# Diagonal matrices in the transposes of the first 12 attention units, and six instead of five weight steps per unit

## The chip, the cores and the metric

The kernel runs on one core of a Trainium2 chip. Its time is what the device needs for one execution, in microseconds (us). The engines of the core work side by side, each through its own queue in order: TensorE (PE in the profile; its weight loads are shown apart as PEld), VectorE (DVE), ScalarE (ACT), GpSimd (POOL) and SyncE (SP, which here only issues transfers).

## The reference

Top-32 attention over 8 batches, 8 heads, 576 positions and head size 64, then a SwiGLU block on the 4608 rows of 512 that it gives. All that is computed:

```python
scores = scale * np.matmul(q, k.transpose(0, 1, 3, 2))
kth = np.partition(scores, -top_k, axis=-1)[..., -top_k:-top_k + 1]
scores = np.where(scores >= kth, scores, -1000000000.0)
scores = scores - np.max(scores, axis=-1, keepdims=True)
attn = np.exp(scores)
attn = attn / (np.sum(attn, axis=-1, keepdims=True) + 1e-09)
x = np.matmul(attn, v)                    # then heads side by side: (4608, 512)
g = x @ w_gate                            # 512 x 1536
y = (g / (1 + np.exp(-g)) * (x @ w_val)) @ w_out
```

The three weight matrices come as 64-bit floats and are rounded to 32 bits on the chip.

## The kernel before

**Units.** The attention is cut into 160 units in this order: batch, block of 128 queries, pair of heads. There are four pairs (`NHP` = 4) and five query blocks for a batch, the last of 64 queries; a unit of that last block counts as one head, since two units share the 128 partitions. So a batch has 16 full units and 4 of one head, and units 0 to 11 are the first three query blocks of batch 0.

**One turn of the main loop** (`for n in range(NU + 3)`) works on several units at once:

- `select(n)`, on DVE: for each head four rounds of MAX8 (L347) with three MATCH_REPLACE8 between them (L351), 14 instructions for a full unit. It writes the working tile `e` of the unit, of which there are three; so unit n waits until unit n-3 has been transposed.
- `weigh(n-1)`, on ACT: Prelu (L374) and Exp (L379) make the unnormalized weights `e` and their sums `tot`; the exponent's offset comes from `shift` on POOL (L362).
- `normalize(n-1)`: the reciprocal of the sums on DVE (L393), then `e` times that reciprocal. For the first 12 units POOL does it for both heads (L399, two instructions of 128x576); from unit 12 on ACT takes the first head (L397).
- `turn(n-2)`, on PE: nine transposes of 128x128 into PSUM (L412), in chunks of four, one and four; the one in the middle holds the last 64 keys of both heads. ACT copies the chunks to the tile `et` (L413).
- in even turns `scores(n+1)` and `scores(n+2)` (PE L325, ACT L330) and, between them, `values` of units n-4 and n-3 (PE L448, ACT L465, which writes `xT`, the input of the feed-forward block).

**The feed-forward block** works on 18 blocks of 256 rows. The first three (`HALVED`) are computed in halves of 128 rows (L517; L569 is the output product of block 0). Its matmuls are put between the attention's steps in pieces: `share(n)` says how much a turn may issue, and `piece()` gives a piece or nothing. A piece of the first two blocks is given only when its weights are ready (`sure`) and its tokens are done.

**Weights.** There are 36 pieces of weights, each of 128x512. Each takes three steps: a transfer from HBM into one of four buffers `w`; three passes on ACT (L117, L119, L120); then a shift on DVE (L124) and two passes on POOL (L125, L126). The generator `weights()` interleaves them, so that a piece is finished by every second step. `dve(k)` lets DVE's selection proceed and, while the six selection instructions of its last three calls go by, adds to `due`; a step of the weights is issued when `due` reaches 1. With 5/6 for each of the six that is five steps per full unit, so 2 or 3 pieces by turns.

**Order.** Nothing is scheduled by a planner. At the end the kernel ties each instruction of PE, DVE, ACT and POOL to the one before it on the same engine, so each of these runs in the order in which the program emits. SP's queue is not tied; its transfers stand in the order of the built program.

Of the kernel before, what the change touches and what calls it, by code (L numbers as in the profile page):

```python
# [9 lines left out]
ALU = mybir.AluOpType  # L10
FP32 = mybir.dt.float32
# [4 lines left out]
P = 128  # L16
# [9 lines left out]
def kernel(  # L26
# [37 lines left out]
    nc = tc.nc  # L64
    B, H, S, D = q.shape
    DM, DFF = w_gate.shape
    J = S // P
    JP = J * P
    R = S - JP
    NHP = H // 2  # L70
# [4 lines left out]
    NBLK = B * S // BLK  # L75
    HALVED = 3
    AHEAD = 8 * NHP
    scale = 1.0 / float(D) ** 0.5
    assert D == 64 and R == 64 and H * D == DM and DM == 512 and B * S % BLK == 0

# [6 lines left out]
    ffn = ctx.enter_context(tc.tile_pool(name="ffn", bufs=2))  # L87
# [3 lines left out]
    ident = consts.tile([P, P], FP32, name="ident")  # L91
# [113 lines left out]
    def rounding(n):  # L205
        for _ in range(n):
            next(weight, None)
# [74 lines left out]
    state = {}  # L282

    def n_heads(qt):

        return 1 if qt == J else 2

    def scores(n):
        b, qt, hp = units[n]
        slab = preps[b * NHP + hp]  # L290
        sc = work.tile([P, 2 * S], FP32, tag="sc", name="sc", bufs=3)
        halves = [slice(0, D), slice(D, P)]
        half = S // 2

        def bank():
            return ps_t.tile([P, 512], FP32, tag="t", name="s")


        if qt == J:
            both = (slab, preps[b * NHP + hp + 1])  # L300
            banks = []
            for i in range(2):
                k0 = R + i * half
                two = [bank(), bank()]
                banks += [(i + 2 * u, ps) for u, ps in enumerate(two)]
                for u, (sl, ps) in enumerate(zip(both, two)):
                    for hh, d in enumerate(halves):
                        nc.tensor.matmul(  # L308
                            ps[halves[hh ^ u], 0:half],
                            sl[d, S + R : S + 2 * R],  # L310
                            sl[d, k0 : k0 + half],
                        )
            yield
            for i, ps in banks:
                nc.scalar.mul(sc[:, i * half : (i + 1) * half], ps[:, 0:half], scale)
            state[n + 1] = dict(sc=sc, at=S)
        else:
            q0 = S + 2 * R + qt * P
            banks = []
            for i in range(2):  # L320
                for hh, d in enumerate(halves):
                    ps = bank()
                    banks.append((i + 2 * hh, ps))
                    k0 = (1 - hh) * R + i * half
                    nc.tensor.matmul(  # L325
                        ps[:, 0:half], slab[d, q0 : q0 + P], slab[d, k0 : k0 + half]
                    )
            yield
            for i, ps in banks:
                nc.scalar.mul(sc[:, i * half : (i + 1) * half], ps[:, 0:half], scale)  # L330
        state[n] = dict(sc=sc, at=0)

    def select(n):

        nh = n_heads(units[n][1])
        sc = state[n]["sc"]
        m = small.tile([P, 2, TOP_K], FP32, tag="m", name="m")
        heads = [slice(t * S, (t + 1) * S) for t in range(nh)]
        at = state[n]["at"]
        from_ = [slice(at + t * S, at + (t + 1) * S) for t in range(nh)]  # L340
        e = work.tile([P, 2 * S], FP32, tag="e", name="e", bufs=3)
        state[n] |= dict(m=m, e=e, heads=heads, source=from_)
        cur = sc
        rounds = TOP_K // 8
        for r in range(rounds):
            for t, hs in enumerate(from_):
                nc.vector.max(m[:, t, 8 * r : 8 * r + 8], cur[:, hs])  # L347
                yield
            if r < rounds - 1:
                for t, hs in enumerate(heads):  # L350
                    nc.vector.match_replace(  # L351
                        e[:, hs], m[:, t, 8 * r : 8 * r + 8], cur[:, from_[t]], LOWEST
                    )
                    yield
                cur, from_ = e, heads
# [11 lines left out]
    def weigh(n):  # L367
# [10 lines left out]
        for t, hs in enumerate(heads):  # L378
# [3 lines left out]
            )  # L382
        if n < AHEAD:
            nc.scalar.add(tot[:, 0 : len(heads)], tot[:, 0 : len(heads)], EPS)
        st["tot"] = tot

    def normalize(n):
        st = state[n]
        tot, e, heads = st.pop("tot"), st["e"], st.pop("heads")
        nh = len(heads)  # L390
        for t in range(nh if n >= AHEAD else 0):
            nc.vector.tensor_scalar_add(tot[:, t : t + 1], tot[:, t : t + 1], EPS)
        nc.vector.reciprocal(tot[:, 0:nh], tot[:, 0:nh])  # L393
        yield
        for t, hs in enumerate(heads):
            if t == 0 and n >= 3 * NHP:
                nc.scalar.mul(e[:, hs], e[:, hs], tot[:, t : t + 1])  # L397
            else:
                nc.gpsimd.tensor_tensor(  # L399
                    e[:, hs], e[:, hs], tot[:, t : t + 1].to_broadcast([P, S]), ALU.mult  # L400
                )

    def turn(n):

        last = units[n][1] == J
        e = state[n].pop("e")
        et = work.tile([P, 2 * J + 1, P], FP32, tag="et", name="et")
        for c0, cn in ((0, J), (J, 1)) if last else ((0, J), (J, 1), (J + 1, J)):
            ps = ps_t.tile([P, 512], FP32, tag="t", name="etps")
            for c in range(cn):  # L410
                k0 = S - P if last and c0 == J else (c0 + c) * P
                nc.tensor.transpose(ps[:, c * P : (c + 1) * P], e[:, k0 : k0 + P], ident[:])  # L412
            nc.scalar.copy(  # L413
                et[:, c0 : c0 + cn, :],
                ps[:, 0 : cn * P].rearrange("p (c j) -> p c j", c=cn),
            )
            if c0 == J:
                yield
        state[n]["et"] = et
# [67 lines left out]
    def flush(queue):  # L487
        while queue:
            queue.pop(0)()
# [314 lines left out]
    def fetch(n):  # L804

        b, qt, hp = units[n]
        i = b * NHP + hp
        if qt == 0:
            yield from prep(i)
        if qt == J and i + NHP < len(pairs):  # L810
            load(i + NHP)

    def share(n):
# [9 lines left out]

        beside = 5.8 if n < AHEAD else 6.25
        least = 2.0 if n >= 3 * NHP and n % 2 == 0 else 0.0
        return max(least, beside * n_heads(units[n][1]) / 2 - others)

    def scored(n):

        ahead = [n + 1] if n < 2 else [] if n % 2 else [n + 1, n + 2]  # L830
        return [m for m in ahead if m < NU and (units[m][1] < J or m % 2 == 0)]
# [11 lines left out]
    def run(steps):  # L843
        for _ in steps:
            pass
# [23 lines left out]
    due, steps = [2.0], []  # L869
    for n in range(NU + 3):  # L870
        nh = n_heads(units[n][1]) if n < NU else 1
        topk = select(n) if n < NU else no
        norm = normalize(n - 1) if 0 <= n - 1 < NU else no
        nxt = [scores(m) for m in scored(n)]
        ahead = fetch(n + 3 if n else 2) if n + 3 < NU else no

        def dve(k, beside=True):

            for _ in range(k * nh):
                next(topk, None)  # L880
                due[0] += 5 / 6 if beside else 0
                if due[0] >= 1 and not (n == 0 and len(steps) == 5):
                    due[0] -= 1
                    steps.append(n)
                    rounding(1)

        if n >= NU - NHP:
            credit[0] = 8.0
        else:
            credit[0] = min(credit[0] + share(n), share(n) + 1)  # L890
        flush(on_act)
        flush(on_pool)
        if nxt and (n < 2 or len(nxt) > 1):
            run(nxt.pop(0))
        summed = finish_units(valued(n)) if valued(n) else no
        next(summed, None)
        if nxt:
            next(nxt[0])
        early[0]()
        if 0 <= n - 1 < NU:  # L900
            weigh(n - 1)
        run(summed)
        if nxt:
            run(nxt.pop())


        dve(2, beside=False)
        if n == 0:
            run(ahead)
            load(3)  # L910
            ahead = fetch(3)
        if n < NHP:
            load_v(n)
        pieces(2)
        flush(on_act)
        dve(1)
        dve(1)
        if 0 <= n - TURN < NU:
            run(turn(n - TURN))

        flush(on_pool)
        next(ahead, None)
        pieces(1)
        next(ahead, None)
        dve(1)
        pieces(1)
        if n < AHEAD:
            run(topk)
        run(norm)
        run(topk)  # L930
        if n < NU:
            shift(n)
        pieces(6)
# [50 lines left out]
```

## Time and profile before

| what | value |
|---|---|
| median of 3 runs | 1713.59 us (1713.14 to 1713.67) |
| profiled execution | 1712.03 us |
| its span, first to last instruction | 1710.2 us |
| PE busy | 1647.4 us, 96% |
| DVE busy | 1476.5 us, 86% |
| ACT busy | 1259.5 us, 74% |
| POOL busy | 799.0 us, 47% |
| mean granted clock of PE | 0.978 |

A row of the tables by line gives the line, the engine, the operation, the tiles, the count, the busy time and the mean of one. A row of the timeline gives the start, the length, the engine, the line and, in brackets, the idle time before it and what ended it. PE is shown in records: a transpose of `e` is one record, a matmul of 32-bit data is two. Turn n ends on DVE with the reciprocal of unit n-1; in the first stretch those stand at 34.5, 44.9, 56.6, 67.3, 79.1, 89.4, 100.8, 111.8, 123.4, 135.8, 148.6, 160.5 and 172.3 us for n = 1 to 13.

### The profile page before, as it was taken

The numbers are of one execution on the slowest core, as the hardware profiler recorded it, in microseconds if no ns is written. First come the engines' busy times: TensorE is split into PE (matmuls) and PEld (weight loads), VectorE is DVE, ScalarE is ACT, GpSimd is POOL, SyncE is SP. The second block draws the span as 40 slices with busy tenths as digits, with TensorE's granted clock in tenths as the row PEclk, the third lists the DMA queues.
The fourth block names the chain that finished last, engine by engine and source line by source line (L and its number), as shares of the span: only waits on it lengthen the run. The fifth ranks groups of instructions, "written<-read, shape, count | busy, mean of one in ns | idle before, by whom it ended". The sixth has DMA issues, their size and how long they took to land.

```text
span 1710.2 us, 32128 instructions
## 1 busy us (share of the span) xinstructions
PE 1647.4 (96%) x11600; PEld 1398.2 (82%) x11600; DVE 1476.5 (86%) x3311; ACT 1259.5 (74%) x2901; POOL 799.0 (47%) x914
## 2 busy tenths in 40 slices
PE   5588999999999999999999999999999999999999
PEld 3477698987888887888888888888888888888887
DVE  7999899998989899997999989998999979999400
ACT  7899887877767787768676887777777778676531
POOL 4798545352444425353535334444344433535434
PEclk6699999999999999999999999999999999999999
DMA  7533120003000030001200030000400011000000
GB/s 210 139 112 99 29 72 2 14 1 79 22 13 1 15 86 14 1 8 42 51 14 1 13 74 27 2 13 2 98 1 13 2 44 29 13 2 13 1 13 13
DMA packets 109310, 59.74 MB, mean 35 GB/s; under 512 B 88544, under 2 KB 96992, under 8 KB 109152
## 3 DMA queue, kind: packets, MB, share of 16 engines
q1 hardware_dynamic: 108016, 57.37, 12.9%
q8 instruction: 91, 1.49, 0.4%
q14 instruction: 67, 0.55, 0.1%
q10 hardware_dynamic: 1136, 0.33, 0.1%
HBM read 48.23 MB, written 9.44 MB: 34 GB/s over the span
## 4 chain that ended last, share of the span: by engine, by line
PE 88%; DVE 5%; ACT 4%; DMA 1%; POOL 1%; issue 1%; SPq 0%; POOLq 0%; ACTq 0%
PE f L604 37%; PE x_ps L670 10%; PE av L448 9%; PE s L325 8%; PE y_ps L670 8%; PE etps L412 7%; PE f L517 6%; DVE m L347 2%; DVE e L351 2%; PE kqps L271 1%; PE o_ps L569 1%; PE s L308 1%; ACT e L379 1%; DVE size L124 1%; ACT e L374 0%
## 5 line engine op out<-in xcount | busy, mean ns | idle before, releaser
L347 DVE MAX8 m<-e 128x8 f32<-128x576 f32 x864 | 617.9, 755 | 3.3
L351 DVE MATCH_REPLACE8 e<-m,e 128x576 f32<-128x576 f32 x576 | 425.4, 748 | 0.0
L604 PE MATMUL f<-xT,wg 128*128 128x256 f32 x1440 | 335.9, 382 | 1.3 <-ACT xT L465 1.3
L604 PE MATMUL f<-xT,wv 128*128 128x256 f32 x1440 | 331.4, 380 | 0.0
L604 PEld LDWEIGHTS f<-xT,wg 128*128 128x128 f32 x1440 | 268.9, 190 | 49.0 <-issue 13.1
L604 PEld LDWEIGHTS f<-xT,wv 128*128 128x128 f32 x1440 | 268.2, 190 | 37.5 <-issue 3.8
L640 POOL TENSOR_TENSOR h<-h,half_g 128x512 f32<-128x512 f32 x90 | 114.7, 1275 | 349.2 <-ACT h L639 349.2
L330 ACT ACTIVATE sc<-s 128x288 f32<-128x288 f32 x512 | 170.4, 431 | 105.2 <-PE s L325 104.6
L413 ACT COPY et<-etps 128x512 f32<-128x512 f32 (+1 forms) x448 | 183.6, 486 | 66.0 <-PE etps L412 65.6
L379 ACT ACTIVATE e<-e,bias 128x576 f32<-128x576 f32 x288 | 221.7, 780 | 12.7 <-POOL bias L362 9.7
L374 ACT ACTIVATE e<-sc,m 128x576 f32<-128x576 f32 x288 | 212.3, 792 | 0.6 <-DVE m L347 0.5
L351 DVE MATCH_REPLACE8 e<-m,sc 128x576 f32<-128x576 f32 x288 | 212.6, 748 | 0.0
L412 PE MATMUL etps<-ident,e 128*128 128x128 f32 x1312 | 178.2, 280 | 33.7 <-POOL e L399 15.0
L347 DVE MAX8 m<-sc 128x8 f32<-128x576 f32 x288 | 204.0, 747 | 7.5 <-ACT sc L330 7.5
L412 PEld LDWEIGHTS etps<-ident,e 128*128 128x128 f32 x1312 | 156.2, 144 | 54.7 <-POOL e L399 19.2
L645 POOL TENSOR_TENSOR h<-h,val 128x512 f32<-128x512 f32 x90 | 114.8, 1275 | 155.0 <-ACT val L644 152.4
L325 PE MATMUL s<-kqT 64*128 64x288 f32 x1024 | 169.2, 441 | 13.7 <-ACT sc L330 7.5
L399 POOL TENSOR_TENSOR e<-e,tot 128x576 f32<-128x576 f32 x140 | 161.1, 1154 | 28.5 <-DVE tot L393 28.2
L448 PE MATMUL av<-et,v 128*64 128x128 f32 (+1 forms) x2560 | 158.0, 268 | 0.0
L448 PEld LDWEIGHTS av<-et,v 128*64 128x64 f32 x2560 | 137.7, 140 | 5.9 <-ACT kqT L268 2.7
L325 PEld LDWEIGHTS s<-kqT 64*128 64x128 f32 x1024 | 94.2, 190 | 58.3 <-issue 18.4
L397 ACT ACTIVATE e<-e,tot 128x576 f32<-128x576 f32 x148 | 119.1, 805 | 21.7 <-DVE tot L393 21.6
(86 smaller groups left out, 2249.1 us busy)
## 6 DMA issues: line engine op xcount, KB each, us to landing
v<-in_v_dram SPq DMA_DIRECT2D x32, 256.0 KB, 3.3
kq_in<-in_k_dram SPq DMA_DIRECT2D x63, 128.0 KB, 2.8
kq_in<-in_q_dram SPq DMA_DIRECT2D x63, 128.0 KB, 2.9
w<-in_moe_w_gate_dram SPq DMA_DIRECT2D x12, 512.0 KB, 3.8
w<-in_moe_w_val_dram SPq DMA_DIRECT2D x12, 512.0 KB, 3.8
w<-in_moe_w_out_dram SPq DMA_DIRECT2D x12, 512.0 KB, 3.5
out_dram<-o SPq DMA_DIRECT2D x38, 128.0 KB, 2.4
out_dram<-o SPq DMA_DIRECT2D x16, 256.0 KB, 2.5
```

The lines of the kernel that those rows point to most:

```text
L325: nc.tensor.matmul(ps[:, 0:half], slab[d, q0 : q0 + P], slab[d, k0 : k0 + half])
L330: nc.scalar.mul(sc[:, i * half : (i + 1) * half], ps[:, 0:half], scale)
L347: nc.vector.max(m[:, t, 8 * r : 8 * r + 8], cur[:, hs])
L351: nc.vector.match_replace(e[:, hs], m[:, t, 8 * r : 8 * r + 8], cur[:, from_[t]], LOWEST)
L374: nc.scalar.activation(e[:, hs], sc[:, at], AF.Prelu, bias=m[:, t, TOP_K - 1 : TOP_K], scale=-1.0, alpha=SMALL,)
L379: nc.scalar.activation(e[:, hs], e[:, hs], AF.Exp, bias=bias[:, t : t + 1], scale=-1.0 / SMALL, accum_out=tot[:, t : t + 1],)
L399: nc.gpsimd.tensor_tensor(e[:, hs], e[:, hs], tot[:, t : t + 1].to_broadcast([P, S]), ALU.mult)
L412: nc.tensor.transpose(ps[:, c * P : (c + 1) * P], e[:, k0 : k0 + P], ident[:])
L413: nc.scalar.copy(et[:, c0 : c0 + cn, :], ps[:, 0 : cn * P].rearrange("p (c j) -> p c j", c=cn),)
L448: nc.tensor.matmul(av[d, i, 0:ql], weights_, moving, start=c == (0 if last else J), stop=c == (J if last else J - 1),)
L604: nc.tensor.matmul(ps[:, i, :], w[:, kc, m * P : (m + 1) * P], x[:, kc, :], start=(kc == 0), stop=(kc == KC - 1),)
L670: nc.tensor.matmul(ps, lhsT, T[i][m], start=m == 0, stop=m == MQ - 1)
```

## The change

In the first 12 units (`SCALED`) `e` is no longer multiplied by the reciprocal sums. POOL makes two diagonal matrices instead, the identity times the reciprocal of each head (one instruction of 128x256), and the transposes of these units become matmuls of `e` with them, which scale while they transpose. The middle chunk holds keys of both heads, so it becomes two matmuls of 64 columns each. The matrices of four units share one tile, in the slot of the output tile `o`. And `due` gets 1 for each selection instruction, so that a full unit issues six steps of the weights, three pieces, until the 36 pieces are through.

```diff
+    SCALED = 3 * NHP
...
+    scaling = []
+
     def normalize(n):
...
         nc.vector.reciprocal(tot[:, 0:nh], tot[:, 0:nh])
         yield
+        if n < SCALED:
+            if not scaling:
+                scaling.append(ffn.tile([P, 4, 2, P], FP32, tag="o", name="diag", bufs=1))
+            st["diag"] = diag = scaling[0][:, n % 4]
+            nc.gpsimd.tensor_tensor(
+                diag,
+                ident[:].unsqueeze(1).to_broadcast([P, 2, P]),
+                tot[:].unsqueeze(2).to_broadcast([P, 2, P]),
+                ALU.mult,
+            )
+            return
         for t, hs in enumerate(heads):
...
         e = state[n].pop("e")
+        diag = state[n].pop("diag", None)
...
-                nc.tensor.transpose(ps[:, c * P : (c + 1) * P], e[:, k0 : k0 + P], ident[:])
+                at = slice(c * P, (c + 1) * P)
+                if n >= SCALED:
+                    nc.tensor.transpose(ps[:, at], e[:, k0 : k0 + P], ident[:])
+                elif c0 == J:
+                    for t in range(2):
+                        d = slice(t * R, (t + 1) * R)
+                        nc.tensor.matmul(
+                            ps[d, at],
+                            e[:, k0 + t * R : k0 + (t + 1) * R],
+                            diag[:, t],
+                            start=True,
+                            stop=True,
+                        )
+                else:
+                    nc.tensor.matmul(
+                        ps[:, at], e[:, k0 : k0 + P], diag[:, c0 // J], start=True, stop=True
+                    )
...
-                due[0] += 5 / 6 if beside else 0
+                due[0] += 1 if beside else 0
```

## The prediction

> **What bounds the kernel now.** The page's first block gives PE 96% and the clock row shows where the rest is: in the first slices.
>
> ```profile
> PE 1647.4 (96%) x11600; PEld 1398.2 (82%) x11600; DVE 1476.5 (86%) x3311; ACT 1259.5 (74%) x2901; POOL 799.0 (47%) x914
> ...
> PEclk6699999999999999999999999999999999999999
> ```
>
> So I read the busy times by stretch next (after each stretch its length, then PE, PEld, DVE, ACT, POOL).
>
> ```profile
> 0.00:43.00 43.00, 24.20 (x97) 16.08 (x97) 31.07 (x70) 33.21 (x76) 19.78 (x27) 0.68 0.78 209
> 43.00:86.00 43.00, 24.63 (x154) 18.41 (x155) 43.00 (x91) 37.86 (x85) 34.06 (x32) 0.64 0.50 138
> 86.00:128.00 42.00, 34.59 (x305) 31.50 (x306) 42.00 (x90) 38.75 (x85) 38.62 (x33) 0.92 0.38 113
> 128.00:171.00 43.00, 37.04 (x310) 34.36 (x309) 42.14 (x82) 39.84 (x89) 38.03 (x35) 0.92 0.32 99
> 171.00:214.00 43.00, 42.59 (x309) 27.85 (x308) 38.40 (x81) 34.78 (x84) 25.46 (x25) 1.00 0.11 29
> ```
>
> To 128 us DVE is full, ACT and POOL near it, and PE idles. From about 137 us PE is full. There a microsecond of PE is a microsecond of the kernel; before, only what delays DVE and ACT counts. PE's own order in time shows the handover: these are the waits of the transposes.
>
> ```profile
> 110.83 1.85 PE L412 MATMUL etps<-ident,e 128*128 128x128 f32 x9 [3.83 <-ACT xT L465]
> ...
> 117.69 0.89 PE L412 MATMUL etps<-ident,e 128*128 128x128 f32 x4 [2.27 <-POOL e L399]
> ...
> 132.94 2.15 PE L412 MATMUL etps<-ident,e 128*128 128x128 f32 x9 [3.90 <-ACT xT L465]
> ...
> 166.65 0.66 PE L412 MATMUL etps<-ident,e 128*128 128x128 f32 x4 [1.61 <-POOL e L399]
> ```
>
> They are units 6, 7, 8 and 11. After unit 8 PE waits only for unit 11 (1.61 and 0.45), then 1.4 us in three places up to 390 us. The first wait of 3.90 is for ACT, which copies `xT` only after weigh, and it comes late: unit 9 ended on DVE at 123.39, its weigh began at 129.33.
>
> **Up to unit 8: PE is covered, DVE and ACT are not.** A chain row gives nine transposes 0.98 us and sixteen matmuls of the feed-forward block, whose shape (128x128, 32 bit) is that of the new matmuls, 3.59.
>
> ```profile
> 183.85 0.98 PE etps L412 x9
> ...
> 217.39 3.59 PE f L517 x32
> ```
>
> 0.109 us against 0.224. The middle chunk's two matmuls have the shape of `values`: 20 in 2.33 us, 0.117 each. A unit costs 8 x 0.115 + (0.233 - 0.109) = 1.05 us more. Units 0 to 7 lie ahead of unit 8: 8.4 us warm, up to twice that at the low clock (nine transposes took 2.44 at 68.89). PE idles 18.4 us in the second stretch and 7.4 in the third; without that cover it is the 8.4.
>
> In the built order PE has 124 feed-forward matmuls (counted in 128 columns) ahead of unit 8's transposes; it had 88. The 36 x 0.224 = 8.1 us go just where the waits of 3.83, 2.27 and 3.90 stand.
>
> DVE: a full unit now holds three shifts (L124), not two or three by turns. What they took in turns 2 to 5 (us on DVE and how many, after the length):
>
> ```profile
> 34.50:44.90 10.40, 0.84 (x2) 0.50 0.59 155
> 44.90:56.70 11.80, 2.31 (x3) 0.65 0.68 178
> 56.70:67.40 10.70, 1.17 (x2) 0.65 0.41 114
> 67.40:79.10 11.70, 2.29 (x3) 0.50 0.43 122
> ```
>
> With turns 6 to 9 (0.83, 1.89, 1.50, 2.07) two cost 1.09 and three 2.14: the third costs 1.05. Turn 1 has one more (0.4), turns 2, 4, 6, 8 one more each: DVE ends turn 5 2.5 us late and turn 9 4.6. A lone shift takes 0.33, the worst 1.46 (at 52.45, beside a POOL pass), so turn 9's figure lies between 1.7 and 7.3. The Trainium skill (SBUF — State Buffer, "SBUF: two separate sides") says that a Vector operation in a two-port mode and a GpSimd operation lock each other out for a whole instruction. The rows fit that but scatter; were each extra shift behind a whole POOL pass, the five would cost 5 x 1.4 = 7.0, not 4.6. I keep the mean.
>
> ACT: a piece is three passes of 0.56, 1.7 us. Its rows around turn 6:
>
> ```profile
> 78.68 0.68 ACT L117 ACTIVATE size<-w 128x512 f32<-128x512 f32 x1 [0.84 <-DMA w<-in_moe_w_gate_dram]
> ...
> 80.38 1.43 ACT L374 ACTIVATE e<-sc,m 128x576 f32<-128x576 f32 x2
> ...
> 82.54 0.77 ACT L379 ACTIVATE e<-e,bias 128x576 f32<-128x576 f32 x1 [0.73 <-POOL bias L362]
> ```
>
> Weigh of unit 5 starts 1.3 after unit 5 ends on DVE (79.06), so it moves with DVE: +2.5. From there ACT hardly idles until the `xT` copy of turn 10 (132.45): it fills up. In between it gets two more pieces and one more copy of `val`, 3.4 + 0.5 = 3.9. It saves the 0.73: the bias stands behind `normalize` on POOL, and the diagonal takes there what a 128x256 pass takes (L677, 0.73; at most the 1.15 of one L399) in place of 2 x 1.15. So the copy, and unit 8's transposes behind it, come 2.5 + 3.9 - 0.7 = 5.7 us late. Bounds: five pieces and the copy are 8.9 in all; ACT idles 8.2 between 20 us and the copy. All idle used gives 0.7 late, none 8.9. I take 5.7, since the idle lies before the 88 us from which ACT is full. On POOL half a piece more (1.33) against 1.6 less in a unit leaves it as it was, and its queue no fuller. On SP, transfers of weights come forward past a load of V and past the next batch's k and q, and hold these up while they wait for a buffer `w`; V is first read two turns later and that k and q ten: nothing.
>
> **From unit 8 on, where PE sets the time.** Against before, from unit 8's transposes to unit 12's: four units of new transposes, +4.2; feed-forward matmuls, of which the order has 124 against 88 ahead of unit 8 but 248 against 232 ahead of unit 12, 20 fewer, -4.5; and unit 11's wait of 1.61 + 0.45 goes, since its diagonal is ready 1.6 sooner and by the order no weight is left on POOL in turns 12 and 13: -2.1. If that wait stays, it is 2.1 back. Sum -2.4: unit 12 stands at 5.7 - 2.4 = +3.3. The lead of 16 matmuls then stays and brings nothing: `share` gives every turn the same, and at turn 36 both orders have issued all that the finished tokens allow (840 matmuls). There PE idles (0.38 and 1.75), and DVE sets the time. DVE in turn is released by PE through the tile `e`:
>
> ```profile
> 336.31 0.09 DVE L351 MATCH_VALUE_LOAD e<-m,sc 128x8 f32 x1 [1.63 <-PE etps L412]
> ```
>
> The last such release that counts is unit 30's transposes, done at 354.41 + 0.98 = 355.39 where DVE needs them at 356.2: 0.8 to spare. So the kernel is 3.3 - 0.8 = 2.5 us late, and from turn 36 on the orders are equal. The profiled execution's 1712.03 (span 1710.2 and 1.8 around it) becomes 1714.5; it lies 1.56 below the median, so the median goes from 1713.59 to 1716.1.
>
> The Trainium skill (TensorE: Matmul & The Clock Gate, "Terms") calls the transpose mode four times faster for 32-bit data. This trace has 0.224 / 0.109, twice. By a factor of four each unit would cost 9 x 0.327 = 2.9, units 8 to 11 11.8 in place of 4.2, and the kernel would be 10 us late; the measured shape decides.
>
> **Rivals.**
>
> *ACT takes nothing of it into its idle time.* For: it is 92% busy from 86 to 128 us, and a longer set of transposes at the low clock makes its copies of `et` (L413) wait, which already waited 4.1 us. Against: 8.2 us of idle, three of its waits caused by POOL. Lateness 8.9 instead of 5.7, +5.7 in the end; with unit 11's wait kept +7.8: 1719.3 to 1721.4. Not faster on any account.
>
> *The early stage swallows the pieces* (the faster side). If ACT's waits (bias 0.71 and 0.73, buffers 0.99, transfers 0.76 to 1.01, matmuls 2.26) all go, it is 0.7 late at unit 8, and unit 12 stands at -1.7. With the 0.8 to spare that is -2.5, and with the remaining 1.4 of PE's waits -3.9: 1709.7. It decides once the lateness at unit 8 falls below 2.4 + 0.8 = 3.2; from there the kernel is faster. For: POOL is relieved, and pieces that go early leave turns 12 to 14 free (three shifts took 2.37 there). Against: DVE is full in turns 2 to 9 and has 2.5 to 4.6 us more work there whatever ACT does.
>
> *It does not do what it says:* the order has no weight steps left after turn 12 (before: turn 14), so the pieces do come early. That the time does not follow is the forecast.
>
> **Chances.** 0.2%, 3.4 us, is about what a measurement of this kernel can tell from no change. The forecast (0 to +5 us, 1713.6 to 1718.6, as lateness goes from 3.2 to 8.2) gets 0.48, of which 0.31 lies within 0.2% and 0.17 above. ACT's rival gets 0.27, all slower. The faster rival gets 0.25: its price of -3.9 is just past the bound, so 0.15 faster and 0.10 within. Faster 0.15, same 0.41, slower 0.44. The range goes from the faster rival's end, 1709.5, to ACT's with the wait kept, 1721.5.
>
> **What would show it.** The transposes of units 0 to 11 as two records each, with 0.22 us a matmul warm. Turns 5 and 9 end on DVE at about 81.6 and 128.0 (79.1 + 2.5, 123.4 + 4.6); turns 12 and 13 last under 10.4 each, as without shifts. Unit 8's transposes at about 138.6 (132.94 + 5.7), with a wait for ACT before them; no wait for POOL at unit 11; unit 12's (183.69 before) at about 187. PE busy up by 12 x 1.05 = 12.6 us. Wrong: unit 8's transposes before 136 (ACT had room), or PE idling again between units 8 and 12 (a wait I have not seen, about one for one in the time).

## The result and the profile after

The changed kernel takes 1720.76 us (median of 6 runs, 1719.23 to 1721.60); before took 1713.18 (6 runs on the same chip, 1712.07 to 1713.67). The ratio is 1.0045, 95% interval 1.0036 to 1.0055: 7.6 us slower, where the prediction had 2.5. The profiled execution took 1720.62 us, its span is 1718.8; against the profiled execution of before that is 8.6 us.

The page after, with the clock row:

```profile
PE 1659.0 (97%) x11732; PEld 1410.1 (82%) x11732; DVE 1475.9 (86%) x3311; ACT 1258.9 (73%) x2901; POOL 778.4 (45%) x902
...
PEclk7689999999999999999999999999999999999999
```

PE is busy 11.6 us more, near the 12.6 of the prediction. DVE and ACT do the same work as before, POOL 20.6 us less. So the loss is only partly work; the windows of the early stage show the rest (after the length PE, PEld, DVE, ACT, POOL):

```profile
43.00:86.00 43.00, 25.88 (x184) 20.72 (x183) 43.00 (x89) 39.53 (x85) 32.38 (x31) 0.70 0.60 162
86.00:128.00 42.00, 37.70 (x312) 35.42 (x312) 37.12 (x76) 37.25 (x82) 32.11 (x29) 0.89 0.40 124
128.00:171.00 43.00, 39.45 (x332) 34.03 (x331) 36.50 (x77) 36.08 (x83) 32.47 (x30) 0.92 0.20 62
171.00:214.00 43.00, 43.00 (x311) 29.66 (x310) 40.50 (x87) 29.63 (x71) 13.89 (x16) 1.00 0.04 15
```

DVE was full to 128 us and nearly to 171. Now it idles 4.9 and 6.5 us in the second and third of these stretches, although it has more shifts to do there. The waits of DVE for the weights up to 172 us say for whom (total, times, longest; after, then before):

```profile
DVE size L125 <- ACT size L118: 16.5, 5, 6.5
```

```profile
DVE size L124 <- ACT size L117: 4.0, 4, 2.3
```

The timelines of turn 6 show the chain behind the first of the long waits, PE first, then ACT, then DVE:

```profile
82.74 0.71 PE L548 MATMUL f<-xT,wg 128*128 128x128 f32 x4
88.02 5.34 PE L548 MATMUL f<-xT,wg 128*128 128x128 f32 x28 [4.57 <-ACT xT L496]
```

```profile
87.61 0.35 ACT L496 COPY xT<-av 128x256 f32<-128x256 f32 x1
87.87 1.32 ACT L331 ACTIVATE sc<-s 128x288 f32<-128x288 f32 x4
93.40 0.60 ACT L568 ACTIVATE h<-f 128x512 f32<-128x512 f32 x1 [4.22 <-PE f L548]
...
94.89 0.68 ACT L118 ACTIVATE size<-w 128x512 f32<-128x512 f32 x1
```

```profile
95.67 0.97 DVE L125 TENSOR_SCALAR size<-size 128x512 int32<-128x512 int32 x1 [4.88 <-ACT size L118]
```

A feed-forward product waits on PE for the turn's copy of `xT`. ACT's gate (L568) waits for the product, the next piece of weights stands behind the gate in ACT's queue, and DVE's shift, which the sixth step has put into this turn, waits for that piece. Turn 10 repeats it, ahead of unit 8's transposes:

```profile
137.20 0.71 PE L548 MATMUL f<-xT,wg 128*128 128x128 f32 x4
141.46 5.90 PE L548 MATMUL f<-xT,wg 128*128 128x128 f32 x28 [3.55 <-ACT xT L496]
147.20 1.06 PE L441 MATMUL etps<-diag,e 128*128 128x128 f32 x8
148.19 0.44 PE L433 MATMUL etps<-diag,e 128*64 128x128 f32 x4
148.56 1.16 PE L441 MATMUL etps<-diag,e 128*128 128x128 f32 x8
149.55 3.74 PE L548 MATMUL f<-xT,wv 128*128 128x128 f32 x32
```

Of the product that was meant to fill this wait, four records do, two matmuls. The third matmul reads the same copy, and so the remaining 28 records wait. (Of the 16 matmuls, eight read parts of `xT` that were copied in turn 8, but all except two of these stand behind the third; another order was not run.) The 28 then run at the low clock, granted 0.54 on the mean, and take 5.74 us (147.20 less 141.46) where the 32 records at 149.55 take 3.57 at 1.00. From 141.46 on PE has no wait until 215 us.

Lateness against before, by the start of the reciprocals on DVE (us):

| end of turn | 1 | 2 | 4 | 5 | 6 | 9 | 10 | 12 | 13 | 36 | 44 | 160 |
|---|---|---|---|---|---|---|---|---|---|---|---|---|
| predicted | | | | +2.5 | | +4.6 | | | | | | |
| measured | +1.65 | +3.02 | +4.05 | +4.06 | +9.93 | +12.09 | +17.57 | +14.30 | +12.16 | +10.50 | +10.09 | +10.06 |

### The profile page after: what moved, and what is told of

The parts are those of the page before. It is cut to its first block, busy times and chain, and to the rows that moved or that the text cites. A ratio compares the mean times of both kernels' runs of the same rounds, so it can differ in the third digit from the quotient of the medians.

```text
span 1718.8 us, 32380 instructions
## 1 busy us (share of the span) xinstructions
PE 1659.0 (97%) x11732; PEld 1410.1 (82%) x11732; DVE 1475.9 (86%) x3311; ACT 1258.9 (73%) x2901; POOL 778.4 (45%) x902
## 4 chain that ended last, share of the span: by engine, by line
PE 85%; DVE 8%; ACT 4%; issue 1%; POOL 1%; SPq 1%; DMA 0%; POOLq 0%; DVEq 0%; ACTq 0%
PE f L635 36%; PE x_ps L701 10%; PE av L479 8%; PE y_ps L701 8%; PE s L326 7%; PE etps L429 7%; PE f L548 5%; DVE m L348 4%; DVE e L352 3%; PE kqps L272 1%; ACT e L380 1%; PE s L309 1%; DVE size L125 1%; ACT e L375 0%; ACT et L444 0%
## 5 line engine op out<-in xcount | busy, mean ns | idle before, releaser
L635 PEld LDWEIGHTS f<-xT,wg 128*128 128x128 f32 x1440 | 268.4, 190 | 49.7 <-issue 13.1
L326 PE MATMUL s<-kqT 64*128 64x288 f32 x1024 | 166.1, 435 | 12.8 <-ACT sc L331 9.3
L429 PE MATMUL etps<-ident,e 128*128 128x128 f32 x1204 | 156.3, 273 | 6.4 <-ACT e L411 3.5
L429 PEld LDWEIGHTS etps<-ident,e 128*128 128x128 f32 x1204 | 140.0, 141 | 21.9 <-ACT e L411 4.0
L413 POOL TENSOR_TENSOR e<-e,tot 128x576 f32<-128x576 f32 x116 | 133.1, 1147 | 47.2 <-DVE tot L396 43.9
L479 PE MATMUL av<-et,v 128*64 128x128 f32 (+1 forms) x2560 | 153.9, 263 | 0.0
L479 PEld LDWEIGHTS av<-et,v 128*64 128x64 f32 x2560 | 133.8, 137 | 5.9 <-ACT kqT L269 2.7
```

The source lines that it names most:

```text
L326: nc.tensor.matmul(ps[:, 0:half], slab[d, q0 : q0 + P], slab[d, k0 : k0 + half])
L413: nc.gpsimd.tensor_tensor(e[:, hs], e[:, hs], tot[:, t : t + 1].to_broadcast([P, S]), ALU.mult)
L429: nc.tensor.transpose(ps[:, at], e[:, k0 : k0 + P], ident[:])
L479: nc.tensor.matmul(av[d, i, 0:ql], weights_, moving, start=c == (0 if last else J), stop=c == (J if last else J - 1),)
L635: nc.tensor.matmul(ps[:, i, :], w[:, kc, m * P : (m + 1) * P], x[:, kc, :], start=(kc == 0), stop=(kc == KC - 1),)
```

## The experiments

All twelve were compared with the kernel before on their own chip; its median there lay between 1713.25 and 1713.65. The traces give three places: where PE goes on after its last wait of turn 10 (R; where there is no wait, at the product), where it starts unit 12's transposes (U12), and how late turn 44 ends on DVE.

| kernel | median us | ratio to before, interval | R | U12 | U12 less before | turn 44 |
|---|---|---|---|---|---|---|
| before | 1713.2 | | 132.94 | 183.69 | | |
| after | 1720.76 | 1.0045 [1.0036, 1.0055] | 141.46 | 193.62 | +9.93 | +10.09 |
| e1_diag_five | 1716.36 | 1.0015 [1.0006, 1.0024] | 134.02 | 187.12 | +3.43 | +3.51 |
| e2_six_only | 1727.56 | 1.0076 [1.0063, 1.0089] | 145.72 | 198.95 | +15.26 | +15.49 |
| e3_hold10 | 1722.28 | 1.0047 [1.0035, 1.0060] | 141.46 | 193.85 | +10.16 | +10.38 |
| e4_hold6_10 | 1720.84 | 1.0042 [1.0029, 1.0054] | 141.22 | 193.39 | +9.70 | +9.93 |
| e5_no_sign | 1720.00 | 1.0041 [1.0029, 1.0054] | 141.64 | 192.71 | +9.02 | +9.41 |
| e6_diag8_five | 1712.73 | 0.9998 [0.9989, 1.0007] | 134.91 | 186.22 | +2.53 | +2.57 |
| e7_before_copy_first | 1710.14 | 0.9983 [0.9974, 0.9992] | 131.80 | 182.30 | -1.39 | -1.33 |
| e8_after_copy_first | 1715.19 | 1.0010 [1.0001, 1.0019] | 137.39 | 188.83 | +5.14 | +5.32 |
| e9_hold_no_sign | 1719.62 | 1.0033 [1.0021, 1.0044] | 138.94 | 190.50 | +6.81 | +7.15 |
| e10_no_shift | 1718.29 | 1.0027 [1.0017, 1.0037] | 139.19 | 190.34 | +6.65 | +6.82 |
| e11_diag8_copy_first | 1708.85 | 0.9975 [0.9964, 0.9985] | 130.17 | 180.41 | -3.28 | -3.26 |
| e12_scores_late | 1712.75 | 0.9999 [0.9990, 1.0008] | 131.96 | 181.58 | -2.11 | -2.07 |

Two things hold in every row. What unit 12's transposes are late, turn 44 is late too, within 0.4 us: all is decided in the first 200 us. And from R to U12 PE takes 49.6 to 53.2 us, so most of the difference between kernels is R. The lateness stands 0.5 to 3.7 us above the difference of medians (below it, by 1.6, in e12_scores_late alone): each trace is of one execution, and that of before lies 1.2 us under its median.

**The two parts alone.** My first theory was the chain of turns 6 and 10 above.

```diff
# e1_diag_five
-                due[0] += 1 if beside else 0
+                due[0] += 5 / 6 if beside else 0
# e2_six_only
-    SCALED = 3 * NHP
+    SCALED = 0
```

> Diagonals alone, five steps of weights in six (due 5/6). Theory: most of the 7.6 us come from the order that the sixth step makes on PE and ACT in turns 6 and 10: a feed-forward product stands ahead of the transposes, waits for the same copy of xT (4.57 and 3.55 us), runs at a low clock (5.34 and 5.90 us for 28 records against 3.39), ACT's gate waits for it (4.22 and 4.78), the weight pieces behind the gate come late and DVE's shift waits for them (16.5 us in 5 waits after, 4.0 in 4 before). Then this kernel, whose ACT order in turn 10 is that of before, is late only by PE's 4.2 us of units 8 to 11, less what unit 11's wait gives back: 0 to +4, about 1715. Rival: the diagonal products themselves cost it (longer transposes hold up ACT's copies of et, and so everything behind them): +5 to +8, 1718 to 1721.

> Six steps of weights a turn alone, transposes with the identity and both heads scaled on POOL as before. Theory of the order in turns 6 and 10: the two stalls are there, +4 to +7, 1717 to 1720. Rival, the diagonals cost it: -1 to +2, 1712 to 1716; DVE then ends turns 6 and 10 no more than 5 us later than before.

The diagonals alone cost 3.0 us (1716.36 less 1713.35), as the theory had it. The sixth step alone costs 14.2, twice the upper end of the theory's +4 to +7, and far above the rival's range. So the two stalls were not all of it, and the diagonals take back 6.6 of these 14.2: with them POOL has less to do. Without them ACT waits for the bias, which stands behind the scaling in POOL's queue (waits of ACT, 120 to 185 us, of e2_six_only):

```profile
ACT e L380 <- POOL bias L363: 9.5, 4, 3.7
```

In the changed kernel this is 2.8 us in two waits. Up to 145 us, ahead of PE's restart, it is 6.3 us in seven waits, and none in the changed kernel: a gain that the prediction priced at 0.7. That these waits make the whole of the 6.6 is not shown.

**Is it the order in turns 6 and 10?** The feed-forward pieces between weigh and the transposes are held back there.

```diff
# e3_hold10 (e4_hold6_10: n not in (6, 10))
-        pieces(2)
+        if n != 10:
+            pieces(2)
         flush(on_act)
         dve(1)
```

> The changed kernel, but no feed-forward pieces between weigh and the transposes in turn 10 alone (they follow the transposes). Theory: PE takes unit 8's transposes as soon as xT is copied, at about 141.5 in place of 147.2; ACT's gate no longer stands ahead of the weight pieces; DVE ends turn 10 some 5 us earlier; the kernel is 3 to 6 us faster than the changed one, 1715 to 1718. Rival (DVE and ACT are late from the extra pieces, whatever the order): within 1 us of the changed kernel, 1720 to 1721.5.

> The same in turns 6 and 10. Theory: turn 6 ends on DVE about 5 us earlier too; what of that reaches the end depends on the weights being ready, so 6 to 10 us faster than the changed kernel: 1711 to 1715. If turn 6's lateness is taken up again by turn 10's idle time: as with turn 10 alone. Rival: 1720 to 1721.5.

Neither brought anything, and the first theory fell. The order did what it should: in e3_hold10 unit 8's transposes start at 141.46 in place of 147.20, and turn 10 ends on DVE 6.3 us earlier. But PE starts at the same time and has the same work ahead:

```profile
141.46 2.05 PE L441 MATMUL etps<-diag,e 128*128 128x128 f32 x8 [4.28 <-POOL size L126]
143.44 0.70 PE L433 MATMUL etps<-diag,e 128*64 128x128 f32 x4
144.06 2.08 PE L441 MATMUL etps<-diag,e 128*128 128x128 f32 x8
145.93 4.01 PE L548 MATMUL f<-xT,wg 128*128 128x128 f32 x32
```

Now the transposes pay the low clock, 4.47 us for the 2.35 that they take warm, and the product follows. (The named releaser, POOL, is only the last event; the copy of `xT` stands at 140.96.) The 6 us that DVE had lost in turn 10 were not on the path. Without the stall of turn 6 (e4_hold6_10) DVE ends that turn 3.9 us earlier, and by turn 9 only 0.9 of it is left: in turns 7 to 9 it waits for `size` in smaller portions, 4.1 us in 3 waits. So something else set the copy in turn 10: ACT's load or DVE's.

**ACT, DVE, or the place of the copy?** e5_no_sign leaves out the sign pass on ACT for weight pieces 10 to 19, e10_no_shift their shift on DVE; these weights then come out wrong, and only the time is of use. Two kernels move the copy ahead of weigh.

```diff
# e5_no_sign: plain is 10 <= i < 20, the number of the weight piece
-        nc.scalar.sign(high, high)
+        if not plain:
+            nc.scalar.sign(high, high)
# e10_no_shift
-        nc.vector.tensor_single_scalar(bits, bits, 3, ALU.logical_shift_left)
+        if not plain:
+            nc.vector.tensor_single_scalar(bits, bits, 3, ALU.logical_shift_left)
# e9_hold_no_sign: e4_hold6_10 and e5_no_sign together
# e7_before_copy_first (on before), e8_after_copy_first (on after)
+        if n in (6, 8, 10):
+            run(summed)
         early[0]()
         if 0 <= n - 1 < NU:
             weigh(n - 1)
```

> The changed kernel with the sign pass on ACT left out for weight pieces 10 to 19, so those weights lack their sign; nothing else of the order changes. Theory A (ACT paces the early stage: it copied xT in turn 10 at 141.05 where before did at 132.45, and PE, full from there on, carries that to the end): of 10 x 0.57 = 5.7 us less on ACT, at least half reaches that copy and the end: copy at 135.5 to 138.5, 1715 to 1718. Theory D (DVE's extra shifts pace it): turn 9 still ends on DVE within 1 us of 135.5, the copy moves by under 1 us, 1720 to 1721.

> The changed kernel with the same move of the copy in turns 6, 8 and 10. Theory A: in turn 10 the 28 records of the feed-forward product start about 3 us earlier and take 3.4 in place of 5.9, ACT's gate waits under 2 us in place of 4.78, and turn 6 likewise: 4 to 9 us faster than the changed kernel, 1712 to 1717. Theory D: under 2 us, 1719 to 1721.

> The kernel before, with the copy of xT put ahead of weigh on ACT in turns 6, 8 and 10, no diagonals and five steps in six. Theory A: PE gets unit 8's transposes about 3 us (the two weigh passes of each head and the sum) earlier, with under 1 us of idle and at full clock, and the end follows: 3 to 6 us faster than before, 1707 to 1710. Theory D: DVE's turns set the end; the copy is earlier but the end moves by under 1 us, 1712.5 to 1714.5.

Without ten sign passes ACT has 5.7 us less to do, and the copy of turn 10 stands at 141.23 (after: 141.05). ACT's load alone does not set the pace. Moving the copy is worth 5.6 us on the changed kernel (1720.76 to 1715.19), and its trace shows why:

```profile
136.22 1.24 PE L326 MATMUL s<-kqT 64*128 64x288 f32 x8
137.39 3.84 PE L548 MATMUL f<-xT,wg 128*128 128x128 f32 x32
141.06 1.06 PE L441 MATMUL etps<-diag,e 128*128 128x128 f32 x8
```

The product runs without a wait and at full clock, and unit 8's transposes start 6.1 us earlier. DVE, though, ends turn 9 only 0.4 us earlier than in the changed kernel (+11.70 against +12.09). So it is PE's restart that counts. On before the same move brings 3.4 us; PE there waits 3.14 us more, up to 131.80, for ACT to copy the scores (`sc`) out of PSUM.

> The changed kernel with both edits that alone brought nothing: no feed-forward pieces ahead of the transposes in turns 6 and 10, and no sign pass on ACT for weight pieces 10 to 19 (those weights lack their sign). Theory B (DVE and ACT are two limits side by side in turns 6 to 9: without the stall of 4.88 us DVE would be on time but ACT is late, without ACT's load DVE is late by its stall): both together make turn 9 end on DVE 3 to 5 us earlier than the changed kernel, xT of turn 10 is copied at 136 to 139 in place of 141.05, and the kernel is 2 to 5 us faster, 1716 to 1719. Rival (DVE's lateness has another source than these two, POOL or the shifts): within 1 us of the changed kernel, 1720 to 1722.

> The changed kernel with the shift on DVE left out for weight pieces 10 to 19 (their bits are not shifted, so these weights are wrong); POOL takes the pieces as ACT leaves them, and DVE neither works on them nor waits for them in turns 4 to 9. Theory B: DVE ends turn 9 10 us or more earlier than the changed kernel's 135.48; ACT then sets the copy of xT in turn 10: its own load puts it at 135 to 139; the kernel is 2 to 6 us faster than the changed one, 1715 to 1719. If DVE alone set the pace: the copy at 132 or earlier, 7 us or more faster. If ACT alone did: within 1 us of the changed kernel.

What neither held-back pieces nor a lighter ACT did alone, both together do in the trace: the copy of turn 10 at 138.44, unit 12 3.1 us earlier, DVE's turn 9 2.8 us earlier. In time it is 1.1 us, between the ranges of the theory and of the rival, and the intervals overlap. So this rests on one trace; the times alone do not show it. Without DVE's ten shifts the copy stands at 138.79 and the kernel is 2.5 us faster, as expected; but DVE ends turn 9 only 2.6 us earlier, where 10 or more were expected. In that kernel DVE ends turn 5 1.1 us earlier than even before, and then stands still:

```profile
93.08 0.98 DVE L126 TENSOR_SCALAR size<-size 128x512 int32<-128x512 int32 x1 [8.13 <-ACT size L118]
```

It is the chain of turn 6 again: a faster DVE arrives early at a piece that comes when ACT's gate lets it. I read this as two limits side by side, DVE and ACT, in turns 5 to 10: relief of one is mostly waited away at the other. Both kernels still start PE 6 us later than before, so the reading is not proven.

**What of the diagonals costs, and a version that beats both.**

```diff
# e6_diag8_five: e1_diag_five and
-    SCALED = 3 * NHP
+    SCALED = 2 * NHP
# e11_diag8_copy_first: that, and the copy of xT first as above
```

> Diagonals in units 0 to 7 alone, five steps in six. Theory: a unit of diagonals costs PE 2.35 in place of 0.98 us once PE is full, so units 8 to 11 are what made the diagonals alone late (4 x 1.37 = 5.5, less 2.1 for unit 11's wait); without them no loss: -1 to +1, 1712 to 1714. Rival (the diagonals hurt by what they do in the early stage): +2 to +4 stays, 1715 to 1717.

> A version meant to beat both: five steps in six, diagonals in units 0 to 7, and the copy of xT ahead of weigh in turns 6, 8 and 10. The copy alone brought 3 us (1710.14 against 1713.54). Theory: PE still waits 5 us for POOL there in units 4 to 8 ahead of the hand-over; the diagonals of units 0 to 7 take most of that away, but it lies where DVE and ACT set the pace: 0 to 2 us more, 1708 to 1710. Rival: the longer transposes hold up ACT's copies, as in turn 7 of the kernel with eight units of diagonals (DVE 3 us late there), and nothing or less is left: 1710 to 1713.

Plain transposes in units 8 to 11 bring 3.6 us (1716.36 to 1712.73), all that the diagonals had cost; on units 0 to 7, where PE has time, they cost nothing that the medians show. (The trace, 2.6 us late at turn 44, is of an execution 2.1 us above the median.) With the copy moved as well the kernel takes 1708.85 us: 4.8 us faster than before, 11.9 faster than the change. Its trace has PE waiting 3.27 us in turn 10 for the scores' tiles, which the last kernel tried to avoid:

```diff
# e12_scores_late, on e11_diag8_copy_first: in turns 8 and 10
-        if nxt:
+        if nxt and n not in (8, 10):
             next(nxt[0])
...
-        if nxt:
+        if nxt and n not in (8, 10):
             run(nxt.pop())
...
             run(turn(n - TURN))
+        if nxt:
+            run(nxt.pop())
```

> The last version (five steps in six, diagonals in units 0 to 7, copy of xT first in turns 6, 8 and 10) and, in turns 8 and 10, PE's scores of two units on and ACT's copies of them behind the transposes and not ahead of weigh. In that version the transposes wait 3.31 and 3.27 us there for ACT to copy sc, since the scores hold the PSUM tiles. Theory A (from turn 10 on PE is full, and what it waits there is the kernel's): the 3.27 goes, 2 to 4 us faster than the last version, 1705 to 1707. Rival (the wait moves to the scores' copies or to DVE, which needs them two turns later): within 1 us, 1708 to 1710.

The rival was right that the wait moves, but the kernel is slower than its range (1708 to 1710): the gain is lost.

```profile
126.14 0.66 PE L429 MATMUL etps<-ident,e 128*128 128x128 f32 x4 [1.59 <-POOL e L413]
127.25 0.77 PE L429 MATMUL etps<-ident,e 128*128 128x128 f32 x5 [0.45 <-POOL e L413]
127.94 0.76 PE L326 MATMUL s<-kqT 64*128 64x288 f32 x4
131.96 1.11 PE L326 MATMUL s<-kqT 64*128 64x288 f32 x4 [3.26 <-ACT et L444]
```

The transposes now go through, and the scores behind them wait as long, 3.26 us, for ACT to copy the transposes to `et` and so free their PSUM tiles. The wait has only changed its name. Of the 3.9 us between the medians the trace shows 1.2; it is of the fastest of 11 executions, 2.7 us below their median, and the rest I can't place.

## Why the prediction was right and wrong

The sign and the place were right: slower, decided between unit 8 and unit 12. The size was not: 1720.76 lies above the forecast's own 1713.6 to 1718.6, and inside the range of the rival on ACT. Its own sum, with what the two traces give:

| step | predicted | measured | from |
|---|---|---|---|
| PE restarts late in turn 10 | +5.7 | +8.52 | 132.94, 141.46 |
| transposes of units 8 to 11 | +4.2 | +4.22 | 9.40 against 5.18 on PE |
| feed-forward up to unit 12 | -4.5 | -0.74 | 33.45 against 34.19 on PE |
| unit 11's wait for POOL | -2.1 | -2.06 | 1.61 + 0.45, gone |
| unit 12's transposes | +3.3 | +9.93 | 183.69, 193.62 |
| slack up to the end of selection | -0.8 | +0.1 | turn 160, +10.06 |
| last stretch | 0 | -1.4 | clock, see below |
| profiled execution | +2.5 | +8.6 | 1712.03, 1720.62 |

**The feed-forward term failed, by 3.8 us.** The prediction counted 124 matmuls against 88 ahead of unit 8's transposes and said that they go "just where the waits of 3.83, 2.27 and 3.90 stand". Of the last 16, 14 stand ahead of the transposes but behind the same copy of `xT`. An operation fills a wait only if neither it nor one ahead of it needs what the wait is for; the order on one engine does not show that, the tiles they read do. Ahead of PE's restart the change has 110 matmuls, not 124, and the product pays the low clock besides.

**The restart was 2.8 us later than the sum.** The sum was ACT's load, 2.5 + 3.9 - 0.7, and its terms can be read off ACT. Weigh of unit 5 begins at 84.53 against 80.38: 4.15 late, not 2.5. From there to the copy of turn 10 ACT is busy 51.71 us against 47.91: 3.8 more, near the 3.9. It idles 4.81 against 4.16: 0.65 more, not 0.7 less. So the added work was priced right; the lateness that came in from DVE and the idle time were not.

DVE's lateness at turn 5 was 4.06, and at turn 9 12.09 instead of 4.6: 1.65 from turn 1, 5.54 from the shifts of turns 2 to 9 (18.44 us against 12.90), 4.88 from the wait in turn 6. Three things were missed. The third shift falls beside a POOL pass in nearly every turn (it takes 1.43 to 1.45 us in 8 of the turns 2 to 11, 0.97 in the two others); in turn 4 (DVE, then POOL):

```profile
63.78 0.40 DVE L125 TENSOR_SCALAR size<-size 128x512 int32<-128x512 int32 x1
...
65.57 0.41 DVE L125 TENSOR_SCALAR size<-size 128x512 int32<-128x512 int32 x1
...
67.23 1.44 DVE L125 TENSOR_SCALAR size<-size 128x512 int32<-128x512 int32 x1
```

```profile
65.69 1.45 POOL L127 TENSOR_TENSOR wg<-size,w 128x512 f32<-128x512 f32 x1
67.10 1.28 POOL L126 TENSOR_TENSOR size<-size,w 128x512 int32<-128x512 int32 x1
68.46 1.35 POOL L127 TENSOR_TENSOR wg<-size,w 128x512 f32<-128x512 f32 x1
```

It takes 1.44, not the mean of 1.05: it starts just after the POOL pass of 67.10 and ends just after that ends. The rows fit the exclusive lock that the Trainium skill describes (SBUF — State Buffer, "SBUF: two separate sides"), whose price of 1.4 a shift the prediction had set beside its sum and not taken. Then turn 1 ends 1.65 us late, nearly all by waits for ACT (0.75, 1.57 and 2.84 against 0.82, 0.48 and 2.27). And the wait of 4.88 in turn 6 was not in the sum at all: of the pieces added there, the prediction asked what they cost ACT, not what stands ahead of them in its queue. ACT had slack for part of that: its weigh of unit 9 began 5.9 us after DVE ended turn 9 before, and 2.5 after (135.48 to 137.94). So 12.1 on DVE became 8.5 on PE.

**The rival "ACT takes nothing of it"** had 8.9 for the restart, and 8.52 came. Its sum came true: from 20 us to the copy of turn 10 ACT is busy 112.71 us against 103.86, 8.85 more, and idles 8.34 against 8.59. Its reasons did not. The 4.1 us of waits of the copies of `et`, which it leaned on, lie at 184 and 202 us in the trace of before, behind this stage; in the changed kernel these copies wait 0.8 us ahead of the copy of `xT`. What kept ACT's idle time up was the gate, which waits 4.66 us for PE's late product (2.26 before). And ACT's load alone does not set the restart: in e5_no_sign ACT is busy 4.6 us less up to the copy, idles 13.1, and the restart does not move. That the time fell into this rival's range was luck in that sense.

**The transposes** came out as predicted by two errors that cancel. A warm unit takes 2.35 us (149.55 less 147.20), 1.37 more than nine transposes and not 1.05; but before paid about 1.0 for the low clock in unit 8's transposes, which after falls on the product. By 1.37 units 8 to 11 cost 5.5, less 2.06 for unit 11's wait 3.4; e1_diag_five against e6_diag8_five measures 3.6. The factor per matmul is 0.246 against 0.109, 2.3; the four times of the Trainium skill (TensorE: Matmul & The Clock Gate, "Terms") is not what this shape shows.

**Right** were: POOL's wait at unit 11 goes; turns 12 and 13 take 9.70 us each, without shifts; the lead in feed-forward matmuls brings nothing, since PE idles 5.2 us between 385 and 428 us where it idled 2.2.

**Open** stays how the 14.2 us of the sixth step alone divide between POOL's bias and the rest (in its trace 12.8 are there at PE's restart, 15.3 at unit 12), and whether DVE and ACT relieved at once over the whole stage would bring PE's restart back to 133.

## What to carry to other kernels

Before work is booked as filling a wait, ask what that work itself waits for: here the filler needed the same copy, and all but two of its matmuls waited too. Where two engines are both near full and hand pieces to each other in order, price an added piece by what stands ahead of it in the other's queue, and expect that relief of one alone comes back as its wait for the other. The cheap gain lay elsewhere: a copy of 0.35 us that releases PE stood behind 3 us of work that PE did not wait for.

## What the runs showed of the hardware

The same wait does not always cost the same clock. Near the end PE waits 1.78 us for ACT in both kernels, then does five transposes; the 16 records behind them, before and after:

```profile
1643.71 1.12 PE L448 MATMUL av<-et,v 128*64 128x64 f32 x16
```

```profile
1653.78 0.69 PE L479 MATMUL av<-et,v 128*64 128x64 f32 x16
```

In the first the granted clock has fallen to 0.50, in the second it stays at 1.00. It falls in 11 of the 14 traces, for 3.4 us each time, beginning 0.2 to 1.4 us after the wait; in 5 of them early enough that these records take over 1 us. In three (after, e3_hold10, e8_after_copy_first) it does not fall. It makes 1.4 us between before and after, the last stretch of the table above, and so limits what single traces can tell of a change of this size. The Trainium skill (TensorE: Matmul & The Clock Gate, "Part 1: The HAM clock gate") has the clock fall after an idle window of about 3.4 us that runs free of the program; that the phase decides fits these rows, a fall at 1.78 us of waiting does not follow from its figure.
